# Attention and feed-forward decode on one core: 57 of 64 pairs in a hardware loop with the kernel's own semaphores

## The chip, the cores and the metric

The kernel runs on one core of a Trainium2 chip. The metric is the device time of one execution in microseconds; the median of three runs is given. A profile is taken of one further execution, and its span goes from the first to the last instruction on the core's engines.

## The reference, cut to what matters

Two blocks with a residual each: attention over a key/value cache for one new position, then a dense block with a squared ReLU. All arrays are float32.

```python
B, Sq, D = 2, 1, 512
H, Sk, Dh = 32, 8192, 128
F = 1792
q = split_heads(layernorm(x) @ wq)                      # [B, H, 1, Dh]
scores = einsum("bhqd,bhkd->bhqk", q, k_cache) * Dh ** -0.5
o = einsum("bhqk,bhkd->bhqd", softmax(scores), v_cache)
h = x + merge_heads(o) @ wo
a = layernorm(h) @ w1 + b1
out = h + (relu(a) * relu(a)) @ w2 + b2
```

There are B x H = 64 pairs of batch and head. Each has 8192 keys and 8192 values of 128 numbers, 8.39 MB together; the two caches are 537 MB of the 561 MB that the kernel reads.

## The kernel before, in words

**Data.** Each pair's keys and values are one array of 128 rows of 16384 floats (64 KB a row). `ring` in SBUF has three slots of that size. Key and value loads, and those of the four weight matrices, are issued by SP into one queue, in the program's order. WQ is loaded first into the slot that pair 2 takes later; WO, W1 and W2 go into slots at the end, when no more pairs need them.

**Start (lines 64 to 149).** The small array is loaded from ACT's queue, WQ and pairs 0 and 1 from SP's. The layer norm of x is computed, then the queries (L139), which are turned (L146) and spread over 32 columns in `QR` (L148). SP issues the load of pair 2 when the queries' matmuls no longer read WQ.

**One pair (lines 157 to 174, called from the loop at 236).** `scores` makes 16 matmuls into four PSUM banks (L162); DVE takes the maximum, negated, of each row (L164, `NM`); ACT takes the exponentials in place and their sums (L169, `LS`); DVE multiplies the four blocks of values by them with a running sum (L174, four instructions, `AC`). Two PSUM tiles of four banks take turns. When the last of the four has read the slot, SP issues the load of the pair three further on (`load_kv(i + 3)`, L58). The profile counts each matmul call twice, as two MATMULs with a weight load each, so 16 calls are 32 MATMULs and 32 LDWEIGHTS.

**End (lines 219 to 341).** The pairs are joined in three groups, of 32, 30 and 2 pairs (`group`, `weigh`, `join`), with WO's rows of each group (`project`, `add_rows`). The first group is joined after pair 60, the second after pair 61, and the last two pairs at the very end. The last pair's values come in five pieces, W1 in four, W2 in five (`W2_PIECES`). After the last values: sums over the quarters (L299), output projection of the last head (L308), layer norm, the hidden layer in two halves (`hidden`, L315, between them the variance in L321), the transposition (L329), the second matrix (L337), the copy to `res` (L340) and the store (L341).

**What sets the order.** The kernel is written out in full for all 64 pairs in a layer (Tile) that records every access to a buffer and puts semaphore waits on each instruction that needs them. The kernel also fixes a few orders by hand (`tc.issue_after`). The layer lets SP have eight loads under way: a load waits until the one eight before it has landed. At the end it lets SP wait for every semaphore, then all five engines meet, the semaphores are cleared, and the engines meet again (all of it is line 367 in the profile).

## Time and profile before

| | |
|---|---|
| median of three runs | 1309.52 us (1309.21 to 1309.79) |
| the profiled execution's own time | 1310.04 us |
| its span, first to last instruction | 1308.3 us |
| outside the span in that execution | 1.7 us |
| read from HBM | 561.00 MB, 429 GB/s over the span |
| PE, DVE, ACT busy | 417.7, 728.9, 145.0 us |
| granted TensorE clock, mean | 0.643 |
| slice-by-slice DMA share, 40 slices | 9 (90% or more) in 39, 7 in the last |

How to read it: the first part of the page gives busy times by engine, the second cuts the span into 40 slices with a digit for the busy tenths, the third lists the DMA queues with packets, bytes and the share of the 16 DMA engines' time. The fourth follows the work that ended last back from the end: at each step to what released it. The fifth lists groups of instructions with their count, busy time, mean duration in ns and the idle time before them; the sixth the DMA issues with the time from issue to landing. A load has landed when the last of its rows has. Lines named SPq are SP's queue instructions.

### The profile page before, as it was taken

The numbers are of one execution on the slowest core, as the hardware profiler recorded it, in microseconds if no ns is written. First come the engines' busy times: TensorE is split into PE (matmuls) and PEld (weight loads), VectorE is DVE, ScalarE is ACT, GpSimd is POOL, SyncE is SP. The second block draws the span as 40 slices with busy tenths as digits, with TensorE's granted clock in tenths as the row PEclk, the third lists the DMA queues.
The fourth block names the chain that finished last, engine by engine and source line by source line (L and its number), as shares of the span: only waits on it lengthen the run. The fifth ranks groups of instructions, "written<-read, shape, count | busy, mean of one in ns | idle before, by whom it ended". The sixth has DMA issues, their size and how long they took to land.

```text
span 1308.3 us, 6011 instructions
## 1 busy us (share of the span) xinstructions
PE 417.7 (32%) x2438; PEld 114.7 (9%) x2438; DVE 728.9 (56%) x626; ACT 145.0 (11%) x152; POOL 0.7 (0%) x6
## 2 busy tenths in 40 slices
PE   2423223323323323322322332332332332332446
PEld 0100000000000000000000000000000000000113
DVE  0464665564565565565566466556456556556553
ACT  1111011011011011011101101101101101101111
POOL 0000000000000000000000000000000000000000
PEclk9666667566656666666656666756665665665766
DMA  9999999999999999999999999999999999999997
GB/s 417 417 447 425 439 433 431 441 425 443 425 439 423 441 429 435 433 435 432 433 431 435 430 437 431 435 431 433 431 437 429 437 429 437 428 439 429 426 426 313
DMA packets 12122, 561.44 MB, mean 429 GB/s; under 512 B 1472, under 2 KB 1600, under 8 KB 2752
## 3 DMA queue, kind: packets, MB, share of 16 engines
q1 hardware_dynamic: 11952, 561.06, 99.3%
q8 instruction: 19, 0.31, 0.1%
q14 instruction: 7, 0.06, 0.0%
q10 hardware_dynamic: 144, 0.01, 0.0%
HBM read 561.00 MB, written 0.07 MB: 429 GB/s over the span
## 4 chain that ended last, share of the span: by engine, by line
DMA 62%; DVE 20%; PE 12%; ACT 4%; another core or an unknown queue 1%; issue 1%; SPq 0%; ACTq 0%
DMA ring<-in_kvd 62%; DVE ring L174 16%; PE s L162 11%; DVE NM L164 4%; ACT s L169 4%; PE s L315 0%; PE s L337 0%; PE s L308 0%; DVE yT L329 0%; PE s L189 0%; PE s L321 0%; PE s L327 0%; SPq L58 0%; PE s L326 0%
## 5 line engine op out<-in xcount | busy, mean ns | idle before, releaser
L162 PE MATMUL s<-ring,QR 128*32 128x512 f32 x2048 | 373.1, 895 | 827.1 <-DMA ring<-in_kvd 718.9
L174 DVE SCALAR_TENSOR_TENSOR ring<-ring,s 128x2048 f32<-128x2048 f32 x252 | 561.5, 2284 | 133.6 <-ACT s L169 133.6
L164 DVE TENSOR_REDUCE NM<-s 128x1 f32<-128x2048 f32 x64 | 146.6, 2291 | 383.4 <-PE s L162 383.4
L169 ACT ACTIVATE s<-s,NM 128x2048 f32<-128x2048 f32 x64 | 124.3, 1942 | 1072.5 <-DVE NM L164 1072.5
L162 PEld LDWEIGHTS s<-ring,QR 128*32 128x32 f32 x2048 | 93.3, 156 | 1104.4 <-issue 1100.9
L174 DVE DVE_READ_ACCUMULATOR ring<-ring,s 128x1 f32 x252 | 20.9, 83 | 0.0
L99 DVE TENSOR_REDUCE part<-sm 128x2 f32<-128x8 f32 x1 | 0.2, 160 | 21.9 <-DMA sm<-in_small 21.9
L169 ACT ACTIVATION_READ_ACCUMULATOR s<-s,NM 128x1 f32 x64 | 12.3, 193 | 0.0
L139 PE MATMUL s<-ring,xn 128*2 128x512 f32 x64 | 9.5, 749 | 1.5 <-ACT rstd L117 0.8
L174 DVE SCALAR_TENSOR_TENSOR ring<-ring,w,s 128x2048 f32<-128x2048 f32 (+1 forms) x5 | 9.6, 1916 | 0.6 <-DMA ring<-in_kvd 0.4
L207 PE MATMUL s<-ring,OT 128*2 128x512 f32 x62 | 8.5, 682 | 3.8 <-DMA ring<-in_wod 3.5
L148 DVE TENSOR_SCALAR QR<-s 128x2048 f32<-128x2048 f32 x1 | 2.3, 2291 | 12.4 <-PE s L146 12.4
L104 PE MATMUL s<-part,ones_d 128*128 128x2 f32 x2 | 0.6, 348 | 23.2 <-DVE hT L132 23.2
L189 PE MATMUL s<-lw,pick_all 128*128 128x32 f32 (+2 forms) x6 | 1.9, 393 | 14.9 <-DVE lw L188 14.9
L315 PE MATMUL s<-ring,xc 128*2 128x448 f32 x32 | 6.3, 942 | 0.6 <-ACT rstd L117 0.4
L181 PE MATMUL s<-NM,pick 128*128 128x32 f32 (+2 forms) x24 | 4.0, 309 | 7.1 <-DVE hT L217 4.6
L95 ACT ACTIVATE s<-zero 128x512 f32<-128x512 f32 (+2 forms) x6 | 3.2, 538 | 19.8 <-DVE OT L201 10.7
L337 PE MATMUL s<-ring,a 128*2 128x128 f32 x112 | 4.7, 348 | 1.5 <-DVE a L334 1.5
L181 PEld LDWEIGHTS s<-NM,pick 128*128 128x128 f32 x24 | 3.7, 236 | 8.9 <-issue 8.9
L117 ACT ACTIVATE rstd<-s,eps_t 128x2 f32<-128x2 f32 x2 | 0.5, 262 | 32.1 <-PE s L128 20.0
L337 PEld LDWEIGHTS s<-ring,a 128*2 128x2 f32 x112 | 3.3, 107 | 3.1 <-DVE a L334 2.0
L340 DVE COPY res<-s 128x128 f32<-128x128 f32 x1 | 0.3, 292 | 4.9 <-PE s L337 4.9
(74 smaller groups left out, 45.3 us busy)
## 6 DMA issues: line engine op xcount, KB each, us to landing
ring<-in_kvd SPq DMA_DIRECT2D x3, 4096.0 KB, 32.4
ring<-in_wod SPq DMA_DIRECT2D x2, 4096.0 KB, 41.8
ring<-in_w1d SPq DMA_DIRECT2D x4, 896.0 KB, 20.3
ring<-in_kvd SPq DMA_DIRECT2D x3, 1024.0 KB, 38.2
ring<-in_w2d SPq DMA_DIRECT2D x2, 1024.0 KB, 16.2
ring<-in_kvd SPq DMA_DIRECT2D x2, 512.0 KB, 38.0
ring<-in_kvd SPq DMA_DIRECT2D x62, 38.8
ring<-in_w2d SPq DMA_DIRECT2D x1, 768.0 KB, 16.8
```

Of the source, the lines that this page charges most:

```text
L95: return nc.scalar.activation(ap, zero.to_broadcast([P, n]), AF.Copy)
L139: nc.tensor.matmul(bk[k][32 * j : 32 * j + B, :], xn[:, d, :], WQ[:, d, n * BLK : (n + 1) * BLK], start=(d == 0), stop=(d == DB - 1))
L148: nc.vector.tensor_scalar(QR, bk[2][:, :BH, None].to_broadcast([P, BH, 32]), SCALE, None, op0=ALU.mult)
L162: nc.tensor.matmul(bk[n][32 * j : 32 * j + 32, :], QR[:, i, :], keys(i)[:, j, n * BLK : (n + 1) * BLK], start=True, stop=True)
L164: nc.vector.tensor_reduce(NM[:, i : i + 1], s, axis=AX.X, op=ALU.max, negate=True)
L169: nc.scalar.activation(s, s, AF.Exp, bias=NM[:, i : i + 1], scale=1.0, accum_out=LS[:, i : i + 1])
L174: return nc.vector.scalar_tensor_tensor(v, v, by, s[:, lo:hi], op0=ALU.mult, op1=ALU.mult, accum_out=acc)
L181: nc.tensor.matmul(pn[:, j], pick[:, j, :], NM[:, a:b], start=True, stop=True)
L189: nc.tensor.matmul(pl[:, :nb], pick_all, lw, start=True, stop=True)
L207: nc.tensor.matmul(hp[32 * j : 32 * j + B, :], OT[:, h * B : (h + 1) * B], WO[:, h, :], start=(h - h0 < NQ), stop=(h1 - h <= NQ))
L315: mm = nc.tensor.matmul(y[32 * j : 32 * j + B, :], xc[:, d, :], W1[:, d, j * FQ : (j + 1) * FQ], start=(d == 0), stop=(d == DB - 1))
L337: nc.tensor.matmul(o[32 * j : 32 * j + B, :], a2[:, m, :], W2[:, m, j * P : (j + 1) * P], start=False, stop=(m == FB - 1))
```

## The change

The recording layer goes. The kernel does the same arithmetic with the same instructions on the same engines, with these differences:

The core of it:

```diff
-    for i in range(last):
-        s = scores(i)
-        exponentials(i, s)
-        for e in range(NH):
-            weighted(i, s, e, 0, CS, AC[:, i, e : e + 1])
-        if i + 3 < last - 1:
-            load_kv(i + 3)
...
+    def take(engine, sem, n=1):
+        engine.wait_ge(sem, n).then_inc(sem, -n)
+
+    loop_engines = [ENGINE.PE, ENGINE.DVE, ENGINE.Activation, ENGINE.SP]
+    with nc.Fori(0, LOOPED, SLOTS, engines=loop_engines, head_slot={e: 0 for e in loop_engines}) as i0:
+        for u in range(SLOTS):
+            k = u % 2
+            s, bk = S[k], banks(k)
+
+            if k == 0:
+                take(pe, s_free)
+            take(pe, kv_full[u], 16)
+            for n in range(CS // BLK):
+                for j in range(NQ):
+                    made = pe.matmul(bk[n][32 * j : 32 * j + 32, :], q3[:, u, :], keys(u)[:, j, n * BLK : (n + 1) * BLK],
+                                     start=True, stop=True)
+            made.then_inc(s_full, 1)
+
+            nm, ls = st3[:, u, 0:1], st3[:, u, 1:2]
+            take(dve, s_full)
+            dve.tensor_reduce(nm, s, axis=AX.X, op=ALU.max, negate=True).then_inc(m_full, 1)
+            if u == SLOTS - 1:
+                dve.tensor_scalar(q3, QT[:, bass.ds(i0 + SLOTS, SLOTS), None].to_broadcast([P, SLOTS, 32]), 1.0, None,
+                                  op0=ALU.mult)
+
+            take(act, m_full)
+            act.activation(s, s, AF.Exp, bias=nm, scale=1.0, accum_out=ls).then_inc(e_full, 1)
+
+            take(dve, e_full)
+            for e in range(NH):
+                v = values(u)[:, e]
+                made = dve.scalar_tensor_tensor(v, v, 1.0, s, op0=ALU.mult, op1=ALU.mult,
+                                                accum_out=st3[:, u, 2 + e : 3 + e])
+            made.then_inc(v_done, 1)
+            take(dve, v_done)
+            dve.tensor_scalar(ALL[:, bass.ds(i0 + u, 1)], st3[:, u : u + 1], 1.0, None,
+                              op0=ALU.mult).then_inc(kv_free, 1)
+
+            take(sp, kv_free)
+            if k == 0:
+                sp.sem_inc(s_free, 1)
+            sp.dma_start(slot(u), kvd[bass.ds(i0 + (SLOTS + u), 1)].rearrange("o p c -> p (o c)")).then_inc(kv_full[u], 16)
...
     def hidden(ds):
         for d in ds:
             for j in range(NQ):
-                mm = nc.tensor.matmul(y[32 * j : 32 * j + B, :], xc[:, d, :], W1[:, d, j * FQ : (j + 1) * FQ],
-                                      start=(d == 0), stop=(d == DB - 1))
-        return mm
-
-    var = sums[:, 384 : 384 + B]
-    with tc.issue_after(hidden(range(2)).ins):
-        mm = nc.tensor.matmul(var, ones_d, squares(xc), start=True, stop=True)
-    rstd = scale_of(var)
-    with tc.issue_after(mm.ins):
-        hidden(range(2, DB))
+                line.matmul(y[32 * j : 32 * j + B, :], xc[:, d, :], W1[:, d, j * FQ : (j + 1) * FQ],
+                            start=(d == 0), stop=(d == DB - 1))
+
+    hidden(range(2))
+    var = hp[:, 384 : 384 + B]
+    line.matmul(var, ones_d, squares(xc))
+    scale_of(var)
+    hidden(range(2, DB))
...
-    nc.sync.dma_start(out, res)
+    line.op("sp", lambda e: e.dma_start(out, res), [res], [], load=True)
+    line.op("sp", lambda e: e.nop(), [], [res])
+    line.flush()
+    sems = range(line.first, nc.alloc_semaphore("end").num + 1)
+    sp.sem_clear(sems)
...
-    with tile.TileContext(nc) as tc:
-        attention_block_kernel(tc, *args)
+    attention_block_kernel(nc, *args)
```

## The prediction

> **What bounds the kernel now.** I read the page first, for whether any engine or the queue is ever without work.

> ```profile
> span 1308.3 us, 6011 instructions
> ...
> PE 417.7 (32%) x2438; PEld 114.7 (9%) x2438; DVE 728.9 (56%) x626; ACT 145.0 (11%) x152; POOL 0.7 (0%) x6
> ...
> DMA  9999999999999999999999999999999999999997
> ...
> q1 hardware_dynamic: 11952, 561.06, 99.3%
> q8 instruction: 19, 0.31, 0.1%
> q14 instruction: 7, 0.06, 0.0%
> ...
> DMA 62%; DVE 20%; PE 12%; ACT 4%; another core or an unknown queue 1%; issue 1%; SPq 0%; ACTq 0%
> ...
> L162 PE MATMUL s<-ring,QR 128*32 128x512 f32 x2048 | 373.1, 895 | 827.1 <-DMA ring<-in_kvd 718.9
> ...
> L148 DVE TENSOR_SCALAR QR<-s 128x2048 f32<-128x2048 f32 x1 | 2.3, 2291 | 12.4 <-PE s L146 12.4
> ```

> The DMA engines carry loads in every slice; DVE, the busiest engine, is at 56%, and PE stands idle 718.9 us until keys land. Two small queues carry the program itself: 0.31 MB in 19 packets, 16 KB each, and 7 packets of 8 KB. PE's 2 x 2438 instructions over 0.31 MB are 64 bytes each, 256 to a packet of q8 (an estimate from these rows); q14 is then DVE's and ACT's, 128 to a packet.

> Next I read the chain in order of time, for the rhythm of the landings (a row "issue" of 0.14 before PE's scores begins when the load has landed; columns: start, us, what).

> ```profile
> 48.43 14.20 another core or an unknown queue
> 62.63 0.14 issue
> ...
> 547.06 0.14 issue
> ...
> 605.11 0.14 issue
> 605.24 6.37 PE s L162 x32
> 611.63 2.30 DVE NM L164
> 613.96 2.07 ACT s L169 x2
> 616.05 8.93 DVE ring L174 x8
> ...
> 625.04 39.09 DMA ring<-in_kvd
> 664.13 0.14 issue
> ...
> 1032.79 0.14 issue
> ...
> 1090.83 0.14 issue
> ...
> 1207.92 0.14 issue
> ```

> From 547.06 to 605.11 three loads landed in 58.05 us, 19.35 each; from 605.11 to 664.13 three took 59.02, 0.97 more. Pair 1 lands at 62.63 and pair 60 at 1207.92: 1145.29 us for 59 loads, where 59 x 19.35 would be 1141.65. So **3.6 us of excess** stand in a stream that is never empty. What came between? The DMA view, cut to these stretches (packets, MB, share of 16 engines), for 605 to 664 (where q8 has no row):

> ```profile
> q14 instruction: 1, 0.01, 0.0%
> ```

> for 1033 to 1091, where three loads took 58.04 and q14 has no row:

> ```profile
> q8 instruction: 1, 0.02, 0.1%
> ```

> and for 62 to 1208:

> ```profile
> q8 instruction: 14, 0.23, 0.1%
> q14 instruction: 7, 0.06, 0.0%
> ```

> One instruction packet of q14 goes with 0.97 us; one of q8 goes with nothing. My reading: a load lands when the slowest of its 16 engines is through, engines work off their rows without a pause, so a packet on the slowest engine delays every later landing, and one on an engine that is ahead costs nothing yet. Were the packets' delay even over the engines, 21 packets at about 1 us would make 21/16 = 1.3 us; the 3.6 is more, so some engine takes about four of them. That the packets are the cause is inferred from two stretches; it is the step most worth testing.

> **The change, part by part.**

> *Code that is fetched.* A round has 3 x 16 matmul calls, 192 PE instructions by the counting above, and by the new program some 40 on DVE: both fit one packet's worth (256 and 128), and the loop's head is laid at the start of a block. If what is fetched stays, the loop needs no packet from about 45 us to its exit, near 1150. Of the 21 packets between 62 and 1208 I keep one or two, for the code behind the loop. The excess of 3.6 goes to between 0 and 0.97 (one packet of the row above, on the slowest engine); I take 0.6, between them. **Gain 3.0 us** at pair 60's landing, bounds 2.6 and 3.6. From there everything is tied to landings, as the tail's rows will show, so it passes through whole.

> *The branch and the loop's waits.* No row of before shows a branch taken back. Its cost lies between nothing and whatever the cover takes. A pair holds its slot 0.14 + 6.37 + 2.30 + 2.07 + 8.93, with the gaps 19.9 us; the load issued then lands 39.09 us later, of which its own transfer is 19.35, so it stands nearly 20 us behind the load before it. Everything that the loop adds on that path is free below some 19 us a pair. On that path come: the third PSUM user of a round (the next round's first scores wait until the third pair is done and SP has said so, 19.9 after a landing against the next landing at 19.35, so 0.6 late, plus some tenths), DVE's copy of six columns behind a wait for itself, the copy into `q3`, and waits as instructions of their own. The nearest row for the copies is one of 128x512 on DVE, larger than both:

> ```profile
> L86 DVE COPY pick<-ident 128x512 f32<-128x512 f32 x1 | 0.4, 419 | 0.0
> ```

> Two copies at 0.42 and the 0.6 stay under 2 us. Behind a DVE that waits stand the next pair's maximum and then SP's load; with 2.30 + 8.93 busy of 19.35, DVE catches up within the pair. Cost: nothing, and no gain either, since the landings set the pace; if the cover were gone, up to 2 us x 57 = 114.

> ```profile
> SPq L58 <- DVE ring L174: 1129.7, 59, 25.4
> ...
> SPq L367 <- PEq L367: 0.6, 2, 0.4
> ```

> The waits of SP's queue: SP has nothing to do but wait for DVE, 1129.7 us of it, so the wait moved to `kv_free` and the counter's arithmetic delay no other issue. A load with an address from a register isn't in this trace: bounded by nothing and by 1% of a load's 19.35, taken as nothing since the rows that it moves are the same (a rival below).

> *The prologue.* `QR` in one 2.29 us instruction becomes three small ones, at most 2 us earlier. The first scores start at pair 0's landing, so 0. Should the jump into the loop cost microseconds, pair 0 alone is late, under the same 19 us.

> *The tail.* Rows of the chain, then of SP's timeline and of the DMA issues:

> ```profile
> 1283.33 0.49 DVE ring L174
> ...
> 1294.15 0.53 PE s L321 x2
> ...
> 1295.03 3.17 PE s L315 x16
> ...
> 1300.51 4.78 PE s L337 x112
> 1305.31 0.29 DVE res L340
> ```

> ```profile
> 1280.89 7.47 SPq L264 DMA_DIRECT2D ring<-in_w2d  x5
> 1305.63 0.35 SPq L341 DMA_DIRECT2D out<-res  x1
> ```

> ```profile
> ring<-in_w2d SPq DMA_DIRECT2D x1, 256.0 KB, 15.2
> out<-res SPq DMA_DIRECT2D x1, 64.0 KB, 1.5
> ```

> DVE's third block of the last values starts when it lands, at 1283.3, and 22 us of dependent work follow. Each engine's order there, by the new program, is that of before, and loads still wait for the one eight before. One edit counts: the second half of `hidden` starts after the variance matmul (1294.15 + 0.53) and not after ACT (1295.03). **Gain 0.3**, bounds 0 (if W1's last piece is what comes late) and 0.35. The other waits, the bank of `po` and the order of `rl` are some hundredths each, either sign. The clock on PE in this stretch is a coin toss that I leave in the range:

> ```profile
> 1290.00:1299.00 9.00, 8.39 (x54) 2.54 (x54) 0.66 (x4) 0.26 (x1) 0.00 (x0) 0.50 0.96 398
> ```

> At a granted 0.50 both halves of `hidden` took 3.17; at full clock up to 3.2 us could go, but W2's last piece, issued at about 1288.0, lands 15.2 later at 1303.2, and a fourteenth of L337's 4.78 follows it: 1303.5 in place of 1305.3, so the clock can't give more than about 1.7.

> *The end.* `res` is ready at 1305.60, the store is issued at 1305.63 and lands 1.5 us later, about 1307.1, and the span ends at 1308.3: 1.2 us, of which 0.6 is meeting (L367 on PEq) and the rest waits and the clearing. One wait and one clearing stay, between 0.1 and 0.5; I take 0.3. **Gain 0.9**.

> Sum: 3.0 + 0.3 + 0.9 = 4.2. The profiled execution took 1310.04, 1.74 over its span, which nothing in the change touches; it goes to 1305.8. That execution stood 0.52 over the median of 1309.52; so **1305.3**.

> **The rivals.**

> *Code is not the cause* (0.14). If the excess has another source, such as the memory, only 0.3 and 0.9 go: 1308.3. For it: a q8 packet went with nothing. Against: 59.02 and 58.04, with and without a q14 packet. [...]

> *The round fetches its code again* (0.11, the other side). Then the loop doesn't do for the queue what I say: 19 rounds bring 19 DVE packets, and if they keep falling on the slowest engine, as one did at 605 to 664, 19 x 0.97 = 18.4 us replace the 3.6: 1309.5 + 18.4 - 3.6 - 1.2 = 1323. It decides from 5 hits: 5 x 0.97 is the 4.8 to be gained, and from 8 it is slower by over 0.2%. With only PE's packets, on engines that are ahead, about 1309. For it: a taken branch is new here. Against: both bodies fit a packet. [...]

> *Loads with a register address are slower* (0.04). Nothing here shows one; 0.08 us a load over 57 loads cancels the gain of 4.2; 1% of 19.35 a load, 57 x 0.19 = 11.0, would give 1309.5 + 11.0 - 4.2 = 1316.

> **How the numbers follow.** 0.2% of 1309.5 is 2.6 us, about what a measurement of this kernel tells from no change. Forecast 0.68 (0.66 of it faster by more than that), code not the cause 0.14 (same), refetching 0.11 (0.09 slower, 0.02 same), register addresses 0.04 (slower), the rest, as a larger saving or losses in the tail by a few tenths, 0.03 (0.02 faster, 0.01 same). Sum: faster 0.68, same 0.19, slower 0.13. The range: low 1309.5 - 3.6 - 0.35 - 1.2 - 1.7 = 1302.6; high is the first rival with its 0.6 of spread, 1308.9. The two slow rivals stay outside, 0.15.

> **What would show it.** Right: q8 and q14 with no packet between the loop's entry and 1150, and three loads at 58.05 to 58.1 throughout; pair 60 about 3 us earlier; SP still waiting for DVE nearly all the time; the store's landing within 0.5 us of the span's end. Wrong: instruction packets at each round's end (then rival two, and the landings say on which engines); landings that step up without packets (rival one); three loads over 58.3 us in the loop with a digit under 9 in the DMA row (issue late, the cover is gone); a tail that keeps 22 us or more after the last values' landing although pair 60 came earlier, which would put my error there.

## The result, and the profile after

The changed kernel takes **1304.93 us** (median of 7 runs, 1304.72 to 1305.29) against 1309.52 (median of 7, 1308.84 to 1310.16). The ratio is 0.9965 with a 95% interval of 0.9953 to 0.9976; the difference of the medians is 4.6 us. The forecast was 1305.3.

The page of the kernel after, its first three parts:

```profile
span 1303.4 us, 6675 instructions
...
PE 425.8 (33%) x2438; PEld 114.9 (9%) x2438; DVE 739.8 (57%) x704; ACT 144.8 (11%) x152; POOL 0.7 (0%) x6
...
DMA  9999999999999999999999999999999999999998
...
q1 hardware_dynamic: 11952, 561.06, 99.7%
q8 instruction: 5, 0.08, 0.0%
q14 instruction: 8, 0.06, 0.0%
```

The work is the same: the same matmuls, the same 561.06 MB in the same 11952 packets, DMA at 9 in every slice but the last. DVE has 11 us more of copies. What changed is the program's own traffic: 5 packets of 16 KB on q8 in place of 19. Those of 8 KB on q14 are no fewer, 7 in both (the eighth in the row is a tiny one), but they come at other times: six between 37 and 48 us, where the loop is entered, and one at 1280, in the epilogue. The DMA view between 60 and 1145 us has a single row, so the loop fetches nothing at all:

```profile
q1 hardware_dynamic: 8089, 470.62, 100.2%
```

PE's timeline gives the landings, 0.14 us before the scores of a pair that waits for nothing else (start, duration). Pair 1, then three loads apart in the middle, then pair 60:

```profile
63.05 1.93 PE L312 MATMUL s<-ring,q 128*32 128x512 f32 x8 [13.82 <-PEq L299]
```

```profile
991.88 5.89 PE L312 MATMUL s<-ring,q 128*32 128x512 f32 x32 [11.50 <-PEq L299]
1011.24 6.45 PE L312 MATMUL s<-ring,q 128*32 128x512 f32 x32 [13.47 <-PEq L299]
1032.22 6.20 PE L312 MATMUL s<-ring,q 128*32 128x512 f32 x32 [14.53 <-PEq L299]
1049.93 5.88 PE L312 MATMUL s<-ring,q 128*32 128x512 f32 x32 [11.51 <-PEq L299]
```

```profile
1204.73 2.79 PE L133 MATMUL s<-ring,QR 128*32 128x512 f32 x12 [12.93 <-DMA ring<-in_kvd]
```

From 991.88 to 1049.93 three loads take 58.05; from pair 1 to pair 60, 59 loads take 1141.68, where 59 x 19.35 is 1141.65. The excess of 3.6 us is 0.03. The pair at 1032.22 starts late, 20.98 after the one before it and not 19.35: it is the first of a round, waiting for the PSUM tile of the third. That costs 1.6 us on PE each round and nothing in the landings.

SP's waits show that the cover stands; a wait of the loop's own is put down to the line of `take`:

```profile
SPq L299 <- SPq L299: 1066.7, 57, 20.3
...
SPq L560 <- DMA out<-res: 1.3, 1, 1.3
```

The end of the chain in order of time, and PE's second half of `hidden` from the timeline:

```profile
1283.41 16.80 DMA ring<-in_w2d
...
1300.26 0.62 PE s L133 x16
...
1300.89 0.44 PE s L133 x8
...
1301.36 0.29 DVE res L144
```

```profile
1292.76 1.99 PE L133 MATMUL s<-ring,xc 128*2 128x448 f32 x16
```

After the change the tail is ended by W2's last pieces: PE waits for them. DVE's third block of the last values starts 1.81 earlier than the 1283.33 of before, and without a wait for its landing:

```profile
1281.52 2.35 DVE L155 SCALAR_TENSOR_TENSOR ring<-ring,w,s 128x2048 f32<-128x2048 f32 x1
```

`res` starts at 1301.36, 3.95 earlier than before, and the span ends 2.0 us behind it in place of 3.0.

Step by step, in the two profiled executions (1310.04 and 1304.73):

| stretch | before | after | change | predicted |
|---|---|---|---|---|
| start to pair 60's scores | 1208.05 | 1204.73 | -3.32 | -3.0 |
| from there to `res` | 97.26 | 96.63 | -0.63 | -0.3 |
| `res` to the span's end | 2.99 | 2.04 | -0.95 | -0.9 |
| outside the span | 1.74 | 1.33 | -0.41 | 0 |
| time | 1310.04 | 1304.73 | -5.31 | -4.2 |

The profiled execution of before stood 0.52 over its median and that of after 0.20 under its own, so the medians lie 4.6 apart and not 5.3.

### The profile page after: what moved, and what is told of

Its sections match the earlier page's. It is cut to its first block, busy times and chain, and to the rows that moved or that the text cites. A ratio compares the mean times of both kernels' runs of the same rounds, so it can differ in the third digit from the quotient of the medians.

```text
span 1303.4 us, 6675 instructions
## 1 busy us (share of the span) xinstructions
PE 425.8 (33%) x2438; PEld 114.9 (9%) x2438; DVE 739.8 (57%) x704; ACT 144.8 (11%) x152; POOL 0.7 (0%) x6
## 3 DMA queue, kind: packets, MB, share of 16 engines
q1 hardware_dynamic: 11952, 561.06, 99.7%
## 5 line engine op out<-in xcount | busy, mean ns | idle before, releaser
L312 PE MATMUL s<-ring,q 128*32 128x512 f32 x1824 | 343.0, 921 | 753.8 <-PEq L299 753.8
L318 DVE TENSOR_REDUCE st<-s 128x1 f32<-128x2048 f32 x57 | 130.6, 2292 | 314.5 <-DVEq L299 314.5
L324 ACT ACTIVATE s<-s,st 128x2048 f32<-128x2048 f32 x57 | 110.7, 1942 | 985.3 <-ACTq L299 985.3
L312 PEld LDWEIGHTS s<-ring,q 128*32 128x32 f32 x1824 | 85.8, 160 | 1009.9 <-issue 1009.9
L133 PE MATMUL s<-ring,QR 128*32 128x512 f32 x224 | 41.0, 898 | 58.3 <-DMA ring<-in_kvd 30.5
L159 DVE TENSOR_REDUCE ALL<-s 128x1 f32<-128x2048 f32 x7 | 16.0, 2291 | 32.8 <-PE s L133 32.8
L137 ACT ACTIVATE s<-s,ALL 128x2048 f32<-128x2048 f32 x7 | 13.6, 1942 | 78.6 <-DVE ALL L159 78.6
L329 DVE DVE_READ_ACCUMULATOR ring<-ring,s 128x1 f32 x228 | 18.7, 82 | 0.0
L333 DVE TENSOR_SCALAR ALL<-st 128x6 f32 x57 | 9.8, 172 | 14.3 <-DVEq L299 14.3
L133 PEld LDWEIGHTS s<-ring,QR 128*32 128x32 f32 x224 | 9.4, 157 | 88.4 <-issue 39.2
L324 ACT ACTIVATION_READ_ACCUMULATOR s<-s,st 128x1 f32 x57 | 11.0, 193 | 0.0
```

The costliest lines, as they stand in the source:

```text
L133: self.op("pe", lambda e: e.matmul(out, lhsT, rhs, start=start, stop=stop), [lhsT, rhs], [out])
L137: self.op("act", lambda e: e.activation(out, in_, func, bias=bias, scale=scale, accum_out=accum_out), [in_, *more], [out] + ([] if accum_o ...
L159: self.op("dve", lambda e: e.tensor_reduce(out, in_, axis=AX.X, op=op, negate=negate), [in_], [out])
L312: made = pe.matmul(bk[n][32 * j : 32 * j + 32, :], q3[:, u, :], keys(u)[:, j, n * BLK : (n + 1) * BLK], start=True, stop=True)
L318: dve.tensor_reduce(nm, s, axis=AX.X, op=ALU.max, negate=True).then_inc(m_full, 1)
L324: act.activation(s, s, AF.Exp, bias=nm, scale=1.0, accum_out=ls).then_inc(e_full, 1)
```

## The experiments

My theory was that code packets on the slowest DMA engine push back every later landing. The main rival was that the lighter semaphores and issue brought the gain and the packets cost nothing. The experiments ran on four chips, with the kernel before beside them on each; there its median was 1308.33 to 1308.87, not the 1309.52 above, so tenths of a microsecond between kernels on different chips tell nothing.

**The loop alone undone** (`unrolled`).

```diff
-    with nc.Fori(0, LOOPED, SLOTS, engines=loop_engines, head_slot={e: 0 for e in loop_engines}) as i0:
+    for i0 in range(0, LOOPED, SLOTS):
```

> The loop alone undone: the 57 pairs written out, the same own semaphores, the same instructions, the same end. Theory (code packets on the slowest DMA engine): DVE runs about 14.7 instructions a pair here, 57 x 14.7 / 128 = 6.5 packets of q14 at 0.97 us each, less the 1.5 that entering the loop adds at the start: pair 60 lands near 1209.4 in place of 1204.6 and the time is 1308.5 to 1310.5, with steps of 0.97 in the landings. Rival (the semaphores and the lighter issue brought the gain): 1304.9, no steps.

1309.58 us (10 runs, 1309.25 to 1310.41), ratio 1.0006 to the kernel before (0.9997 to 1.0016; 1308.87 on this chip). The whole gain is gone, with the own semaphores and the end without a meeting still there. Its timeline on PE, second pairs of three rounds:

```profile
936.70 5.60 PE L312 MATMUL s<-ring,q 128*32 128x512 f32 x32 [11.99 <-PEq L299]
...
994.75 5.59 PE L312 MATMUL s<-ring,q 128*32 128x512 f32 x32 [11.97 <-PEq L299]
...
1053.78 5.09 PE L312 MATMUL s<-ring,q 128*32 128x512 f32 x32 [13.00 <-PEq L299]
```

The first three loads take 58.05, the next three 59.03. The DMA view of the first stretch (937 to 994) has one q8 packet and none of q14:

```profile
q1 hardware_dynamic: 421, 24.51, 99.4%
q8 instruction: 1, 0.02, 0.1%
```

and that of the second (995 to 1053) one q14 packet and none of q8:

```profile
q1 hardware_dynamic: 429, 25.03, 99.8%
q14 instruction: 1, 0.01, 0.0%
```

Pairs 1 and 60 of this kernel:

```profile
61.52 1.93 PE L312 MATMUL s<-ring,q 128*32 128x512 f32 x8 [13.63 <-PEq L299]
```

```profile
1208.60 1.94 PE L133 MATMUL s<-ring,QR 128*32 128x512 f32 x8 [13.73 <-DMA ring<-in_kvd]
```

That is 1147.08 us for the 59 loads, an excess of 5.4, where before had 3.6 and after has 0.03: DVE runs more instructions a pair here than in before (after, which runs the same ones, counts 704 on its page, before 626), and more is fetched, 9 packets of q14 between the two landings in place of 7. The rival falls. Pair 1 is 1.53 earlier here than in the kernel after: that is the price of entering the loop. So of the 5.4 the loop saves 3.9 at pair 60.

**More executed, and more fetched.** Thirteen tiny memsets on DVE per pair, once in the loop (`loop_sets`) and once written out (`unrolled_sets`); and thirteen tiny copies per pair in the kernel before (`before_sets`). The lines that make `idle` are left out.

```diff
+            for c in range(13):
+                dve.memset(idle[:, c : c + 1], 0.0)
             take(dve, e_full)
```

```diff
         exponentials(i, s)
+        for c in range(13):
+            nc.vector.tensor_copy(idle[:, c : c + 1], NM[:, i : i + 1])
```

> The changed kernel with 13 tiny memsets on DVE per looped pair, still one 8 KB packet's worth for the body. Theory: executing more without fetching more costs nothing, 1304.9 within 0.3, no q14 packet in the loop. Rival (DVE's work or its queue time sets the pace): 13 x 0.06 x 57 = 44 us more at most.

> The same 13 memsets with the loop written out: about 27.7 DVE instructions a pair, 12.3 packets of q14. Theory: 12.3 x 0.97 - 1.5 = 10.5 above the changed kernel, 1315.4, between 1313 and 1317. Rival: as the looped one, 1304.9.

> The kernel before with 13 tiny copies on DVE per pair (of the maximum, 128x1): 22.8 DVE instructions a pair, 10.1 packets up to pair 57 in place of 4.4. Theory: 5.7 x 0.97 = 5.5 above the kernel before, 1315. Rival (the excess of 3.6 is the memory's or Tile's waits'): 1309.5, since DVE has 8 us to spare in each pair.

Measured: 1305.84 (10 runs, 1305.01 to 1307.06), 1314.61 (4 runs, 1314.54 to 1314.84; ratio 1.0045, 1.0028 to 1.0061) and 1315.14 (4 runs, 1314.81 to 1315.18; ratio 1.0047, 1.0031 to 1.0064). The same memsets add 5.0 us to `unrolled` (1309.58) and 0.9 to the loop (1304.99 on another chip). In the kernel before the copies add 6.3 to the 1308.87 of that chip, although DVE has room for them (before, it is busy for 728.9 of 1308.3 us). q14's row in the DMA view, 62 to 1145 us, of `before_sets` and then of `unrolled_sets`:

```profile
q14 instruction: 12, 0.10, 0.0%
```

```profile
q14 instruction: 14, 0.11, 0.0%
```

The kernel before has 7 there and `unrolled` 8. The step is the same size as ever. The chain of `before_sets` has three loads in 1155.63 - 1096.61 = 59.02:

```profile
1096.61 0.14 issue
...
1115.61 40.03 DMA ring<-in_kvd
1155.63 0.14 issue
```

`loop_sets` misses its 0.3: it has no packet in the loop (60 to 1145 us), but the one q14 packet that follows the loop falls between 1145 and 1282, ahead of the last values:

```profile
q14 instruction: 1, 0.01, 0.0%
```

In the kernel after, that packet falls between 1279 and 1283, at the last values' pieces:

```profile
q14 instruction: 1, 0.01, 0.5%
```

That the 39 instructions that the body has more shift it is my reading; that this is the whole 0.9 is not shown.

**Which engine the packets hit.** The views print when a load has landed whole. The trace also keeps sixteen landing times of each load, read here as one for each DMA engine. Those of pair 60, sorted, in six kernels (`pool_sets` and `early_heads` follow below):

| kernel | q14 packets, pair 1 to 60 | first | fifteenth | last |
|---|---|---|---|---|
| after | 0 | 1202.65 | 1204.57 | 1204.60 |
| early_heads | 1 | 1202.59 | 1204.62 | 1205.64 |
| before | 7 | 1202.70 | 1206.17 | 1207.92 |
| unrolled | 9 | 1202.61 | 1206.04 | 1208.46 |
| unrolled_sets | 15 | 1202.55 | 1205.94 | 1214.50 |
| pool_sets | 0 (12 more ahead of pair 1) | 1202.60 | 1205.36 | 1211.24 |

The first is the same in all to 0.15, so the loads as a whole are not slower; in all kernels but after, one of the sixteen is behind all others, by 1.02 to 8.56. Followed from load to load, 5 of the 7 packets of q14 in before and 12 of the 15 in `unrolled_sets` hold back this same one, by 0.96 to 1.03 each. A packet of q8 holds back its engine by more, about 1.5 us, but in `unrolled_sets` the 16 of them go round eight others, two each by pair 60, some 3.1 us. They don't show in the landings there, since the one engine is further behind (11.95 from the first to the last, 3.39 to the fifteenth). Without that one engine, before would still land at its fifteenth's 1206.17 (an estimate): that is 1.75 of the gain of 3.3, and the rest goes with q8's packets, which the loop takes away too.

**Packets alone** (`pool_sets`): 1536 memsets on POOL, whose result nobody reads.

```diff
+    idle = sb("idle", 12 * 128)
+    for c in range(12 * 128):
+        line.memset(idle[:, c : c + 1], 0.0, "pool")
```

> The changed kernel with 1536 memsets on POOL, which has nothing to do and nobody waits for: 12 packets of 8 KB early in the run, on POOL's own fetch. It measures where code packets fall. Theory: steps in the landings while POOL fetches and none later; 12 x 0.97 = 11.6 if all fall on the slowest engine (1316.5), 0 to 1.5 if they go round the 16 (1305 to 1306.5). Rival (code packets cost the loads nothing): 1304.9, no step.

1310.49 us (10 runs, 1309.79 to 1311.31), 5.5 over the changed kernel's 1304.99 on another chip. The q14 row of the DMA view up to 75 us has 18 packets of 8 KB, where the kernel after has 7 in the same stretch, six of 8 KB and the tiny one:

```profile
q14 instruction: 18, 0.15, 0.5%
```

Pairs 1 and 60:

```profile
69.78 6.19 PE L315 MATMUL s<-ring,q 128*32 128x512 f32 x32 [16.77 <-PEq L302]
```

```profile
1211.38 1.93 PE L133 MATMUL s<-ring,QR 128*32 128x512 f32 x8 [12.79 <-DMA ring<-in_kvd]
```

Pair 1 is 6.7 us late and pair 60 still 6.7: between them 1141.60, no excess. So here the packets delayed the loads while they came and at no other time, with no engine waiting for POOL. Both sizes that were expected miss: 12 x 0.97 would be 11.6, and going round the sixteen at most 1.5; it is 6.7. By the sixteen landing times they do fall on one engine: at pair 0 fifteen land by 42.02 and the last at 47.60, which also speaks against POOL's writes as such slowing the loads. At pair 60 the last is 8.6 behind the first, where the kernel after has 1.95 from its entry: 6.7 more, 0.56 for each of the 12 packets. Why it is less than 0.97 here is open.

**A body over a block's end** (`dve_straddles`, `pe_straddles`): only the slot of one engine's loop head changes (the loop's line is cut to it).

```diff
-head_slot={e: 0 for e in loop_engines}
+head_slot={e: 230 if e == ENGINE.DVE else 0 for e in loop_engines}
```

```diff
+head_slot={e: 160 if e == ENGINE.PE else 0 for e in loop_engines}
```

> The changed kernel with DVE's loop head at slot 230 of a block, so that its 47 slots cross a block's end. It tells my second rival's price. If a crossing round fetches: 19 to 38 packets of q14, each 0.97 on one engine, 1323 to 1341. If two blocks stay: no packet in the loop, 1304 to 1306.

> The changed kernel with PE's loop head at slot 160, so that its some 200 slots cross a block's end. If a crossing round fetches: 19 to 38 packets of q8; they go round some engines, so 1 to 5 us, 1306 to 1310, and PE's scores of the first pair of a round start microseconds after the landing, which costs nothing. If two blocks stay: 1304.9.

1304.19 (5 runs, 1303.94 to 1305.33) and 1305.04 (7 runs, 1304.55 to 1305.18). In 60 to 1145 us each has one instruction packet, of q14 in the first (between 70 and 90) and of q8 in the second:

```profile
q14 instruction: 1, 0.01, 0.0%
```

```profile
q8 instruction: 1, 0.02, 0.0%
```

One packet in 19 rounds that run over the end of a block: these rounds don't fetch again. That refutes my second rival for bodies of this size, and not for longer ones, which weren't tried.

**The engines meet at the end again** (`end_meets`).

```diff
+    nc.all_engine_barrier()
     sp.sem_clear(sems)
+    nc.all_engine_barrier()
```

> The changed kernel with the meeting of all engines put back around the clearing of the semaphores at the end, twice. Prediction's term: 0.6 to 0.9 above the changed kernel, 1305.5 to 1305.9; the stretch from the store's landing to the span's end goes from 0.1 to about 0.8. Rival (the runtime's own end hides it): 1304.9.

1306.12 us (11 runs, 1305.92 to 1306.73), 1.1 over `pe_straddles` on the same chip, whose pair 60 starts its scores at 1204.96, where `end_meets` has 1204.95. The store of this kernel, in SP's timeline, and its span:

```profile
1302.08 0.35 SPq L556 DMA_DIRECT2D out<-res  x1
```

```profile
span 1304.3 us, 6698 instructions
```

From the store's issue to the end it is 2.2 us, against 1.7 in the kernel after (1301.67 to 1303.4): 0.5. Most of the rest lies outside the span: 1306.09 - 1304.3 = 1.8, as before's 1.74, where the kernels without a meeting have 1.3 to 1.4 (1304.73 - 1303.4, `unrolled` 1309.41 - 1308.0).

**The old wait in the hidden layer** (`hidden_waits`): the second half's matmuls wait for `rstd` again.

```diff
-                line.matmul(y[32 * j : 32 * j + B, :], xc[:, d, :], W1[:, d, j * FQ : (j + 1) * FQ],
-                            start=(d == 0), stop=(d == DB - 1))
+                out, l, r = y[32 * j : 32 * j + B, :], xc[:, d, :], W1[:, d, j * FQ : (j + 1) * FQ]
+                line.op("pe", lambda e, o=out, l=l, r=r, d=d: e.matmul(o, l, r, start=(d == 0), stop=(d == DB - 1)),
+                        [l, r] + ([rstd] if d >= 2 else []), [out])
```

> The changed kernel with the old wait put back: the second half of the hidden layer waits for ACT's square root and the reciprocal after it. Prediction's term: 0.3 above. Rival (the last piece of W2 ends the tail, as the profile after has it): 0, 1304.9. At full clock in the last 10 us I lean to the rival.

1306.72 us, and in two groups: 3 of 11 runs at 1304.82 to 1305.25, 8 at 1306.47 to 1307.09. PE's timeline of the profiled one (1306.72), and of the changed kernel in its later run (`after_again`, below), whose first half starts only 0.33 earlier:

```profile
1295.40 3.17 PE L533 MATMUL s<-ring,xc 128*2 128x448 f32 x16 [0.55 <-DVE rstd L162]
```

```profile
1294.45 1.85 PE L133 MATMUL s<-ring,xc 128*2 128x448 f32 x16
```

The second half took 3.17 here and 1.85 there. The same stretches with the granted clock (the last column but two):

```profile
1295.40:1298.34 2.94, 2.94 (x16) 0.53 (x17) 0.00 (x0) 0.00 (x0) 0.00 (x0) 0.50 0.91 362
```

```profile
1294.45:1296.12 1.67, 1.67 (x17) 0.38 (x17) 0.17 (x1) 0.26 (x1) 0.00 (x0) 0.89 1.01 415
```

The first half ran at 0.50 in both. So the wait itself is 0.55 us on PE, and here the clock stayed at half through the second half too; `res` starts at 1303.41 and not at 1301.58. Whether the gap brings the slow clock is not settled: `early_heads`, on the same chip and without the wait, stood in two groups too. No run of the lower group was profiled here.

**Heads in the first block** (`early_heads`).

```diff
-head_slot={e: 0 for e in loop_engines}
+head_slot={ENGINE.PE: 0, ENGINE.DVE: 48, ENGINE.Activation: 32, ENGINE.SP: 24}
```

> The changed kernel with the loop heads of DVE, ACT and SP in the block in which they start (slots 48, 32 and 24; PE's stays at 0 of its next), so that entering the loop needs no fetch on these three. Theory: the six q14 packets at 38 to 47 us mostly go, the slowest engine lags 0.5 to 1.2 and not 1.94 after pair 0, all later landings come 0.7 to 1.4 earlier: 1303.5 to 1304.2. Rival (the lag at the start is PE's packet alone): 1304.9.

1306.05 (11 runs, 1304.78 to 1306.58): a miss. Entering the loop fetches as much as ever, 6 packets of q14 and one of q8 between 37 and 48 us, the same counts as in the kernel after:

```profile
q1 hardware_dynamic: 80, 4.19, 89.8%
q14 instruction: 6, 0.05, 1.1%
q8 instruction: 1, 0.02, 0.6%
```

So the slots did not put the heads into code that was there already; why not is open. In the profiled run (1305.15, of the lower group) another packet comes at a worse time: the one of q14 that the kernel after has at 1280 comes between 1160 and 1180, ahead of pair 60, whose scores start 1.04 later than there:

```profile
q14 instruction: 1, 0.01, 0.1%
```

```profile
1205.77 5.79 PE L133 MATMUL s<-ring,QR 128*32 128x512 f32 x32 [14.12 <-DMA ring<-in_kvd]
```

One packet, one step. What parts the two groups is not shown.

**The changed kernel again, beside the best variant** (`after_again`, `dve_straddles_again`).

> The changed kernel as it is, beside the next one on one chip. 1304.9 by its earlier runs; if the granted clock in the last 15 us is a toss that also falls the other way here, some of its runs stand 1 to 2 us above the others, as with the kernel whose second half of the hidden layer waits; if that wait alone decides it, all stand within 0.5.

> DVE's loop head at slot 230 again, as a candidate that beats the changed kernel: its epilogue on DVE then crosses no block's end, so the code packet of DVE at 1280.5, which the profile after shows on the slowest engine between two pieces of the last values (0.9 us), is not there. Theory: 0.4 to 0.9 below the changed kernel. Rival (the difference seen before was the chip's): equal.

1304.99 (9 runs, 1304.81 to 1305.38; ratio 0.9974, 0.9964 to 0.9984) and 1304.62 (7 runs, 1304.31 to 1305.13; ratio 0.9970, 0.9959 to 0.9981). With DVE's head at slot 230 the kernel is 0.4 us faster at the median, the least that was expected, and the ranges overlap: it may be a little better, and the runs don't decide it. Its profile has no packet of q14 between 1279 and 1284, where the changed kernel has one in both its profiles. The changed kernel stood in one group on this chip. Here it is 3.3 us faster than the kernel before (1308.33), where the first chip had 4.6: the kernel after took the same, the kernel before less.

## Why the prediction was right

**The code fetch** (3.0 predicted, 3.3 found) is the step that carried it, and it is shown now and not only inferred: taking the loop alone away gives all of it back (1.0006), adding fetched code to the written-out kernels makes them slower, in steps of 0.97 us, executing the same instructions from the loop adds no packet in the loop, packets of an unrelated engine delay the loads by themselves, and the sixteen landing times show that one engine alone is late. I kept 0.6 us for packets behind the loop before pair 60; there was 0.03. What I had not counted is the entry: against `unrolled` its seven packets make pair 1 late by 1.53 us. Against before it is only 0.28: that kernel has a packet of q8 between 42 and 48 us, and its pair 1 comes 20.61 after pair 0 and not 19.35.

"Some engine takes about four of them" was close: it took five, at 0.96 or 0.97. Some 1.2 us of these 4.8 don't show, since the packet of q8 had left another engine 1.1 behind at pair 1. That a q8 packet "goes with nothing" was right for the landings and wrong as a price: it costs its engine 1.5. Since the loop does away with both kinds at once, that did not hurt the sum; by the estimate above, a change that took away q14's packets alone would have brought about 1.75, where the prediction's reading promises the whole.

**The branch, the handshakes and the copies cost nothing**, as predicted. The first pair of a round starts 1.6 us late and not 0.6 and some tenths; the 19 us of cover take it. SP waits 1066.7 us in 57 waits, 18.7 each; it was 1129.7 in 59, 19.1 each.

**Loads with a register address** land at 19.35, as the others did. That rival is gone.

**The tail** (0.3 predicted, 0.63 found): the sign was right and the size not only the wait's. The second half of `hidden` ran in 1.99 in place of 3.17 by the clock, the coin toss left in the range, and it gave no more than 0.63 because W2's last piece then ends the tail, which is the limit the prediction worked out. "It passes through whole" held, but not by the path that was given: the last values moved by 1.81 and not 3.3, DVE no longer waiting for them, and the rest was made up because PE, at the higher clock (0.83 granted in the second half, against 0.50 before), reached W2's landings in time. The packet of q14 at 1280.5 also holds back the last engine by 0.9, and so W2's last pieces.

**The end** (0.9 predicted, 0.95 found in the span). The claim that nothing touches the 1.74 us outside the span was wrong: it fell by 0.4, and `end_meets` brings it back.

**The sum.** With these the profiled executions lie 5.3 apart and not 4.2, and the medians 4.6 on the first chip and 3.3 on the last. The mechanism was right; that the forecast came within 0.4 us of the first median is in part luck.

**The rivals.** The first (code isn't the cause) and the second (a round fetches again) are refuted by `unrolled` and the straddling bodies: a packet that strikes costs 0.97 us, `unrolled` has 5.4 us of excess in all, and the straddling bodies have one packet each in 60 to 1145 us. Against a source other than the program's packets, such as the memory, stands the first of the sixteen landings, at 1202.55 to 1202.70 in the six kernels, while the last goes from 1204.60 to 1214.50.

## What to carry to other kernels

Here the DMA queue never emptied, and the program itself was traffic: the written-out kernels paid for their code in landings (3.6 us of excess in before, 5.4 in `unrolled`), and the loop didn't (0.03, with no packet in 60 to 1145 us, and one where a body ran over a block's end). In a kernel bound by its loads, look for it as landings that step up by a fixed amount (0.97 us here), and set the packets of the instruction queues beside them, stretch by stretch. Waits that ended before the next load was due cost nothing here (1.6 us on PE each round, none of it in the landings), so count first how far the issue stands ahead of the queue.

## What the runs showed that I had not expected

- A packet of 8 KB on q14 cost up to 0.97 us in the landings and one of 16 KB on q8 mostly nothing, though it held its engine for 1.5: most of the first kind fell on one DMA engine (5 of 7 in before, 12 of 15 in `unrolled_sets`), the second went round eight in `unrolled_sets`.
- Code of an engine that nobody waits for cost time: 12 packets of POOL made 6.7 us.
- The meeting of the engines at the end cost 0.5 us within the span and 0.4 outside it.
- With the same work the second half of the hidden layer's matmuls took 1.85 to 1.99 us at a granted 0.89 and 0.83, or 3.17 at 0.50. With a wait of 0.55 us ahead of it, `res` came 1.8 us later; that the clock also parts the runs of one kernel is likely and not shown.
